# An attention and two feed-forward layers with expert routing on one core: the end of routing rearranged

## The chip, the cores and the metric

The kernel runs on one core of a Trainium2 chip. The metric is the device time of one execution in microseconds; the comparison with the kernel before is made by the median of several executions. TensorE (PE) does the matmuls and transposes here; VectorE (DVE), ScalarE (ACT) and GpSimd (POOL) work on the tiles; SyncE (SP) issues transfers. PEld in the profile is TensorE's loading of the stationary operand, which overlaps the matmuls.

## The reference

Three parts follow each other on 2304 tokens of 512 numbers (batch 4, sequence 576).

```
# 1: linear attention with random features, 8 heads
x = attention(q, k, v, omega)
# 2: normalised, gated feed-forward, 1536 wide
xn = x / sqrt(mean(x*x) + 1e-6) * rms_g
y = (silu(xn @ w_gate) * (xn @ w_val)) @ w_out
# 3: eight experts with 288 places each
logits = y @ gate                      # 2304 x 8
order = argsort(-logits.flatten())     # best pairs first
for idx in order: tok, e = idx // 8, idx % 8
    if assigned[tok] < 0 and counts[e] < 288: assigned[tok] = e; counts[e] += 1
for e in range(8): out[assigned == e] = relu(y[assigned == e] @ w1[e]) @ w2[e]
```

Everything is float32; the kernel multiplies with operands split into a high and a low part and takes three products (high by high, high by low, low by high).

## The kernel before

Attention and the first half of the feed-forward layer fill the first 556 us. The logits are known before the feed-forward's output `y` is, since the gate's weights are folded into `w_out`. So from then on two things run interleaved on PE: **routing**, a chain of many short steps that finds for each expert the threshold of its logits, and the **second half of the feed-forward layer**, `ffn2`, a generator that yields after each of its 648 matmuls (18 tiles of 128 tokens, 36 matmuls each, line 880).

Routing (`route`, lines 107 to 266) has seven phases. A phase finds a threshold in six digits; in each digit VectorE compares all logits with candidates (`ge`, line 152), PE counts the hits in 18 small matmuls (`cnt`, line 163), VectorE compares the counts with the room left (`ok`, line 165), one more matmul (line 169) sums the result, and VectorE reads the digit. The first two digits have 62 and 63 candidates, the other four 31. Then follows a settlement (lines 182 to 223). After the phases come the places of the tokens (lines 225 to 257), 18 last matmuls (line 262) and the list `ids` of the tokens of each expert (line 266). Wherever PE would wait for VectorE, `route` yields a number of nanoseconds, and the caller issues that much of `ffn2`, counted at 233 ns a matmul with the fraction carried on:

```
FILL = (5400, 2500, 1900, 466, 1400, 3400, 4500)   # first digit, second, others, ok, settlement, places, last
FILL_MM = 233
```

What is left of `ffn2` when routing ends is issued behind it (line 917). This whole stretch stands in `tc.manual_schedule(engines={PE, DVE})`: its PE and VectorE instructions keep the order in which they are written. Everywhere else a planner, which has a cost model of its own, orders each engine's instructions; every engine and every queue then works strictly in the order so made.

When a tile of `ffn2` is complete, ScalarE copies it out of PSUM into a tile `ws` (line 889) and SP stores it into `y_dr` in DRAM (line 890). SP also issues all loads. For the last two tiles (TAIL) the values are also kept in SBUF, `yt`, as a high part by ScalarE (line 886) and a low part by VectorE (line 887).

The experts work in transposed form. `gather(e, j)` (line 936) fetches 96 tokens of expert e from `y_dr` by an indirect DMA on POOL's queue, three per expert. Those of even experts go into the three tiles named `xh`, those of odd experts into the three named `xl`, of which `yt` and `hot` take up all three until expert 0 has been turned. Expert 0 does not wait for the last two feed-forward tiles: its gather reads only the earlier rows, rows that are not there are set to zero (line 942), and its four turns add the others by matmuls of `yt` with a one-hot matrix `hot` (line 957; `hot` is made on line 1001 from a loaded `iota`). `turn(e, d)` (line 944) transposes a quarter of the columns by PE into a PSUM tile `gv`, of which there are two, and splits it into `exh` by ScalarE (line 959) and `exl` by VectorE (line 960). `layer1` (line 962) makes 12 matmuls of a block of 128 hidden units, lines 968 to 970, and two evacuations (971, 972) out of one of two PSUM tiles; there are eight blocks per expert. `layer2` makes 24 matmuls per block, lines 978 to 980, and there are four blocks. `store` transposes the result back and scatters it to the output.

The experts' weights come in eight pieces of 512 KB per expert. `exp_load` (line 829) loads a piece into one of three `ws` tiles, `exp_split` (line 855) converts it into a high part (ScalarE, line 861) and a low part (VectorE, line 862) in one of twelve `wc` tiles. Six pieces are converted during routing; six `wc` tiles hold `w_out` until `ffn2` ends.

Of the kernel before, what the change touches and what calls it, by code (L numbers as in the profile page):

```python
# [1 line left out]

# [1 line left out]

# [5 lines left out]
F32 = mybir.dt.float32  # L10
# [13 lines left out]
SL = 96  # L24
# [9 lines left out]
W_SCALE = 2.0 ** -112  # L34
DIGITS = (6, 6, 5, 5, 5, 5)
SHIFTS = (26, 20, 15, 10, 5, 0)
FILL = (5400, 2500, 1900, 466, 1400, 3400, 4500)
FILL_MM = 233

DW = 3  # L40
# [239 lines left out]
def kernel(ctx, tc, qT, kT, v1, om, wgv, rms, wo, wg2, w1, w2, cfd, trd, cid, out, dbg=None):  # L280
# [548 lines left out]
    def exp_load():  # L829
        if wcur[0] < len(wseq):  # L830
            e, c = wseq[wcur[0]]
            wcur[0] += 1
            sv = stage.tile([128, 1024], F32, name="ws")
            nc.sync.dma_start(sv, w1[e, c] if c < 4 else w2[e, c - 4])
            wload[e, c] = sv
# [19 lines left out]
    def exp_split(pool, lo):  # L855
        if wcur[1] < len(wseq):
            e, c = wseq[wcur[1]]
            wcur[1] += 1
            sv = wload.pop((e, c))
            w = pool.tile([128, 2, 1024], F32R, name="wc")  # L860
            nc.scalar.copy(w[:, 0], sv)  # L861
            lo.tensor_sub(w[:, 1], sv, w[:, 0])  # L862
            wch[e, c] = w

    def ffn2():
        for i, (c, g) in enumerate(seq2):
            if i + HB - 1 < len(seq2):
                ffn2_load(*seq2[i + HB - 1])
            if i % 6 == 2 and wcur[0] < EARLY:
                exp_load()  # L870
            if i % 6 == 4 and wcur[1] < EARLY:
                exp_early()
            ht = hts.pop((c, g))
            if g == 0:
                py = psB.tile([128, DM], F32, name="py")
            for i4 in range(4):
                f = 4 * g + i4
                w = wos[f // 2].rearrange("p l (i d) -> p l i d", i=2)
                for n, (a, l) in enumerate(((0, 0), (0, 1), (1, 0))):
                    nc.tensor.matmul(py, ht[:, i4, a], w[:, l, f % 2], start=(f == 0 and n == 0),  # L880
                                     stop=(f == KF - 1 and n == 2))
                    yield
            if g == 2:
                t = c - (NC - TAIL)
                if t >= 0:
                    nc.scalar.copy(yt[t][:, 0], py)
                    nc.vector.tensor_sub(yt[t][:, 1], py, yt[t][:, 0])
                ys = stage.tile([128, DM], F32, name="ws")
                nc.scalar.copy(ys, py)  # L889
                nc.sync.dma_start(y_dr[c * 128:(c + 1) * 128, :], ys)  # L890

    yt = [xp.tile([128, 2, DM], F32R, name="xl") for _ in range(TAIL)]
    filler = ffn2()
# [40 lines left out]
    hot = xp.tile([128, TAIL, CAP], F32R, name="xl")  # L934

    def gather(e, j):
        xg[e, j] = xp.tile([SL, DM], F32, name="xl" if e % 2 else "xh")
        rows = ids[:, e * NJ + j:e * NJ + j + 1] if e else idc[:, j:j + 1]
        nc.gpsimd.indirect_dma_start(out=xg[e, j], out_offset=None, in_=y_dr if e else y_dr[:NT - 128 * TAIL, :],
                                     in_offset=bass.IndirectOffsetOnAxis(ap=rows, axis=0))  # L940
        if e == 0:
            nc.vector.tensor_scalar(xg[0, j], xg[0, j], here[:, j:j + 1], None, op0=OP.mult)

    def turn(e, d):

        if d == 0:
            xgt[e] = (sb.tile([128, KD, CAP], F32R, name="exh"), sb.tile([128, KD, CAP], F32R, name="exl"))
        xh, xl = xgt[e]
        pt = psG.tile([128, NJ, SL], F32, name="gv")
        for j in range(NJ):  # L950
            nc.tensor.matmul(pt[:, j, :], xg[e, j][:, d * 128:(d + 1) * 128], ident[:SL, :SL], is_transpose=True,
                             start=(j == 0), stop=(j == NJ - 1), skip_group_check=True)
        pv = pt.rearrange("p j s -> p (j s)")
        if e == 0:
            for t in range(TAIL):
                for l in range(2):
                    nc.tensor.matmul(pv, yt[t][:, l, d * 128:(d + 1) * 128], hot[:, t], start=False,
                                     stop=(t == TAIL - 1 and l == 1), skip_group_check=True)
        nc.scalar.copy(xh[:, d], pv)
        nc.vector.tensor_sub(xl[:, d], pv, xh[:, d])  # L960

    def layer1(e, f, hh, hl):
        xh, xl = xgt[e]
        w = wch[e, f // 2].rearrange("p l (k m) -> p l k m", k=KD)
        m = slice((f % 2) * 128, (f % 2) * 128 + 128)
        ph = ps.tile([128, CAP], F32, name="ph")
        for k in range(KD):
            nc.tensor.matmul(ph, w[:, 0, k, m], xh[:, k], start=(k == 0), stop=False)  # L968
            nc.tensor.matmul(ph, w[:, 0, k, m], xl[:, k], start=False, stop=False)  # L969
            nc.tensor.matmul(ph, w[:, 1, k, m], xh[:, k], start=False, stop=(k == KD - 1))  # L970
        nc.scalar.activation(hh[:, f], ph, AF.Relu)
        nc.vector.scalar_tensor_tensor(hl[:, f], ph, 0.0, hh[:, f], op0=OP.max, op1=OP.subtract)
# [10 lines left out]
    def store(e, j, yT):  # L983
        po = ps.tile([SL, DM], F32, name="po")
        for d in range(KD):
            nc.tensor.transpose(po[:, d * 128:(d + 1) * 128], yT[:, d, j * SL:(j + 1) * SL], ident)
        yo = sb.tile([SL, DM], F32, name="yo", bufs=3)
        nc.vector.tensor_copy(yo, po)
        nc.gpsimd.memset(spacer, 0.0)
        s_ = nc.gpsimd.indirect_dma_start(  # L990
            out=out, out_offset=bass.IndirectOffsetOnAxis(ap=ids[:, e * NJ + j:e * NJ + j + 1], axis=0),
            in_=yo, in_offset=None)
        for t in scat:
            tc.declare_no_dep(s_.ins, t.ins, reason="other rows")
        scat.append(s_)
# [9 lines left out]
    exp_load()  # L1005
    for j in range(NJ):
        gather(1, j)
    for d in range(KD):
        turn(0, d)
    w2pool = ctx.enter_context(tc.tile_pool(name="w2pool", bufs=1))  # L1010
    for n in range(2):
        exp_load()
        exp_split(wpool, nc.vector)

    yprev = None
    for e in range(E):
        hh = sb.tile([128, KE, CAP], F32R, name="ehh", bufs=1)
        hl = sb.tile([128, KE, CAP], F32R, name="ehl", bufs=1)
        yT = sb.tile([128, KD, CAP], F32, name="yT", bufs=2)
        for f in range(KE):  # L1020
            layer1(e, f, hh, hl)
            if yprev is not None and f < NJ:
                store(e - 1, f, yprev)
            if f in (3, 4, 5) and e + 2 < E:
                gather(e + 2, f - 3)
            if f % 2:
                exp_load()
                exp_split(wpool, nc.vector)
        for d in range(KD):
            if e + 1 < E:  # L1030
                turn(e + 1, d)
            layer2(e, d, hh, hl, yT)
            exp_load()
            exp_split(wpool, nc.vector)
        yprev = yT
    for j in range(NJ):
        store(E - 1, j, yprev)
# [46 lines left out]
```

## Time and profile before

| | us |
|---|---|
| median of three executions | 1009.11 (1009.09 to 1012.57) |
| profiled execution, own time | 1010.09 |
| its span from first to last instruction | 1008.2 |
| TensorE busy in the span | 971.8 |
| VectorE, ScalarE, GpSimd busy | 534.5, 399.8, 242.1 |
| first and last matmul of `ffn2` start | 556.1, 762.0 |
| first and last matmul of layer 1 of the experts start | 769.2, 984.8 |

A profile is one execution. Its page gives the busy time of each engine, the chain of work that ended last and the costliest groups of instructions; the trace behind it can be asked for the instructions of a stretch, for one source line, or for sums by window. In brackets behind an instruction stands how long its engine was idle before it and what released it. The times of matmuls overlap, since they are pipelined.

### The profile page before, as it was taken

The page shows a single profiled execution, that of the slowest core. Times are in us where ns is not written, and L with a number is a line of the kernel's source. Part 1 is how long each engine was busy: PE and PEld are TensorE (multiplying, and loading weights), DVE is VectorE, ACT ScalarE, POOL GpSimd, SP SyncE. Part 2 cuts the span into 40 slices and gives each one's busy share as a digit, 9 for nine tenths or more (in the row PEclk, how much of TensorE's full clock was granted, in tenths as well). Part 3 has the DMA queues.
Part 4 walks back from the last instruction along what each step waited for, and adds up shares of the span by engine and source line. Part 5 has one row for each costly group of instructions (what it writes and reads, how often), then busy time and mean ns, then how long its engine had stood idle before and what let it go on. Part 6 is the DMA issues. An engine that isn't in the chain of part 4 may idle for free.

```text
span 1008.2 us, 19316 instructions
## 1 busy us (share of the span) xinstructions
PE 971.8 (96%) x7649; PEld 886.8 (88%) x7649; DVE 534.5 (53%) x1239; ACT 399.8 (40%) x999; POOL 242.1 (24%) x325
## 2 busy tenths in 40 slices
PE   6998899999999999999999999999997999999996
PEld 5888899989989989999999777777776999999996
DVE  3779956544653344432234465555554656665531
ACT  4985546546654544332233100100003644444420
POOL 1345512233344222322223000000005121222111
PEclk7999999999999999999999999999998999999998
DMA  8436752366544211732224466655536755655400
GB/s 274 158 113 207 222 160 81 127 212 200 178 144 148 102 53 49 202 112 83 83 98 156 138 183 203 189 175 161 158 94 213 246 187 189 199 194 193 150 24 24
DMA packets 112074, 153.32 MB, mean 152 GB/s; under 512 B 8560, under 2 KB 78832, under 8 KB 111984
## 3 DMA queue, kind: packets, MB, share of 16 engines
q1 hardware_dynamic: 108768, 142.52, 43.8%
q0 software_dynamic: 3072, 9.44, 2.9%
q8 instruction: 60, 0.98, 0.4%
q14 instruction: 30, 0.25, 0.1%
q10 hardware_dynamic: 144, 0.13, 0.0%
HBM read 108.03 MB, written 44.04 MB: 151 GB/s over the span
## 4 chain that ended last, share of the span: by engine, by line
PE 77%; issue 9%; DVE 6%; DMA 2%; ACT 2%; POOL 2%; SPq 0%; POOLq 0%; DVEq 0%; ACTq 0%
PE py L880 16%; PE gv L595 10%; PE gv L596 9%; PE gv L597 9%; PE pm L457 3%; PE pm L412 2%; PE cnt L163 2%; PE ph L968 2%; PE py L978 2%; PE ph L970 2%; PE ph L969 2%; PE py L979 2%; PE py L980 2%; DVE dw L527 2%; PE pm L453 2%
## 5 line engine op out<-in xcount | busy, mean ns | idle before, releaser
L595 PE MATMUL gv<-xh,wc 128*128 128x256 f32 x864 | 253.5, 294 | 6.4 <-DVE hp L610 6.0
L596 PE MATMUL gv<-xl,wc 128*128 128x256 f32 x864 | 250.1, 289 | 0.0
L597 PE MATMUL gv<-xh,wc 128*128 128x256 f32 x864 | 249.7, 289 | 0.0
L880 PE MATMUL py<-wc,ht 128*128 128x512 f32 x648 | 175.9, 409 | 0.0
L595 PEld LDWEIGHTS gv<-xh,wc 128*128 128x128 f32 x864 | 165.1, 191 | 10.7 <-DVE hp L610 7.0
L596 PEld LDWEIGHTS gv<-xl,wc 128*128 128x128 f32 x864 | 165.4, 191 | 0.8
L597 PEld LDWEIGHTS gv<-xh,wc 128*128 128x128 f32 x864 | 165.4, 191 | 0.6
L880 PEld LDWEIGHTS py<-wc,ht 128*128 128x128 f32 x648 | 114.4, 188 | 21.9
L607 DVE SCALAR_TENSOR_TENSOR th<-th,gv 128x256 f32<-128x256 f32 x108 | 45.1, 418 | 122.6 <-ACT th L606 122.4
L378 ACT ACTIVATE ft<-pp,mx 128x128 f32<-128x128 f32 (+1 forms) x320 | 93.9, 373 | 25.9 <-DVE mx L375 24.7
L620 POOL TENSOR_TENSOR hp<-h,hp 128x256 fp32r<-128x256 f32 x84 | 65.5, 780 | 156.1 <-ACT hp L619 156.0
L862 DVE TENSOR_TENSOR wc<-ws,wc 128x1024 fp32r<-128x1024 f32 x58 | 70.9, 1224 | 32.7 <-ACT wc L861 32.4
L606 ACT ACTIVATE th<-gv 128x256 f32<-128x256 f32 x108 | 41.5, 384 | 105.3 <-PE gv L597 105.0
L968 PE MATMUL ph<-exh,wc 128*128 128x288 f32 x256 | 78.9, 309 | 0.0
L978 PE MATMUL py<-ehh,wc 128*128 128x288 f32 x256 | 78.0, 305 | 0.0
L970 PE MATMUL ph<-exh,wc 128*128 128x288 f32 x256 | 76.2, 298 | 0.0
L969 PE MATMUL ph<-exl,wc 128*128 128x288 f32 x256 | 76.1, 298 | 0.0
L979 PE MATMUL py<-ehl,wc 128*128 128x288 f32 x256 | 75.9, 297 | 0.0
L980 PE MATMUL py<-ehh,wc 128*128 128x288 f32 x256 | 75.8, 296 | 0.0
L375 DVE TENSOR_REDUCE mx<-pp 128x4 f32<-128x512 f32 (+2 forms) x88 | 55.6, 635 | 33.9 <-PE pp L368 21.1
L889 ACT COPY ws<-py 128x512 f32<-128x512 f32 x18 | 10.6, 586 | 145.8 <-PE py L880 132.2
L861 ACT CAST wc<-ws 128x1024 fp32r<-128x1024 f32 x58 | 61.0, 1051 | 3.1 <-DMA ws<-in_w_dram 3.0
(197 smaller groups left out, 1843.2 us busy)
## 6 DMA issues: line engine op xcount, KB each, us to landing
ws<-in_w_dram SPq DMA_DIRECT2D x64, 512.0 KB, 3.4
ht<-h_dr SPq DMA_DIRECT2D x54, 512.0 KB, 4.2
h_dr<-hp SPq DMA_DIRECT2D x42, 512.0 KB, 2.6
ws<-in_wgv_dram SPq DMA_DIRECT2D x24, 512.0 KB, 4.0
ws<-in_wo_dram SPq DMA_DIRECT2D x12, 512.0 KB, 4.3
h_dr<-dw SPq DMA_DIRECT2D x24, 256.0 KB, 2.1
y_dr<-ws SPq DMA_DIRECT2D x18, 256.0 KB, 4.3
vt<-in_v_dram SPq DMA_DIRECT2D x12, 325.0 KB, 4.0
```

Source lines behind the costliest of these rows:

```text
L378: nc.scalar.activation(ft[:n, g], pp[:n, g], AF.Exp, bias=mx[:n, g:g + 1])
L595: nc.tensor.matmul(pg[:, v], w[:, 0, k, v], xh[:, k], start=(k == 0), stop=False)
L596: nc.tensor.matmul(pg[:, v], w[:, 0, k, v], xl[:, k], start=False, stop=False)
L597: nc.tensor.matmul(pg[:, v], w[:, 1, k, v], xh[:, k], start=False, stop=(k == KD - 1))
L862: lo.tensor_sub(w[:, 1], sv, w[:, 0])
L880: nc.tensor.matmul(py, ht[:, i4, a], w[:, l, f % 2], start=(f == 0 and n == 0), stop=(f == KF - 1 and n == 2))
L968: nc.tensor.matmul(ph, w[:, 0, k, m], xh[:, k], start=(k == 0), stop=False)
L969: nc.tensor.matmul(ph, w[:, 0, k, m], xl[:, k], start=False, stop=False)
L970: nc.tensor.matmul(ph, w[:, 1, k, m], xh[:, k], start=False, stop=(k == KD - 1))
L978: nc.tensor.matmul(py, w[:, 0, k], hh[:, k], start=(k == 0), stop=False)
L979: nc.tensor.matmul(py, w[:, 0, k], hl[:, k], start=False, stop=False)
L980: nc.tensor.matmul(py, w[:, 1, k], hh[:, k], start=False, stop=(k == KE - 1))
```

## The change

`FILL` gets smaller portions for the first digit, the second and the others. The store of a finished feed-forward tile is issued by ScalarE, not by SP. The gathers of expert 1 get three tiles of their own, `xe`. An unused pool is dropped. The two conversions of weights in front of the experts' loop are dropped, so that each later one takes the piece two further back. The turns of expert 0 and all of expert 0's matmuls, with those of expert 1's turns among them, are put in the written order on PE; in that order the first two turns of expert 1 stand behind the first block of expert 0's layer 2, not before it. For the other experts the planner orders PE as before.

```diff
--- before.py
+++ after.py
@@ -1,4 +1,4 @@
-from contextlib import ExitStack
+from contextlib import ExitStack, nullcontext
 
 import numpy as np
 
@@ -34,7 +34,7 @@
 W_SCALE = 2.0 ** -112
 DIGITS = (6, 6, 5, 5, 5, 5)
 SHIFTS = (26, 20, 15, 10, 5, 0)
-FILL = (5400, 2500, 1900, 466, 1400, 3400, 4500)
+FILL = (5100, 2450, 1800, 466, 1400, 3400, 4500)
 FILL_MM = 233
 
 DW = 3
@@ -887,7 +887,7 @@
                     nc.vector.tensor_sub(yt[t][:, 1], py, yt[t][:, 0])
                 ys = stage.tile([128, DM], F32, name="ws")
                 nc.scalar.copy(ys, py)
-                nc.sync.dma_start(y_dr[c * 128:(c + 1) * 128, :], ys)
+                nc.scalar.dma_start(y_dr[c * 128:(c + 1) * 128, :], ys)
 
     yt = [xp.tile([128, 2, DM], F32R, name="xl") for _ in range(TAIL)]
     filler = ffn2()
@@ -934,7 +934,11 @@
     hot = xp.tile([128, TAIL, CAP], F32R, name="xl")
 
     def gather(e, j):
-        xg[e, j] = xp.tile([SL, DM], F32, name="xl" if e % 2 else "xh")
+        if e == 1:
+
+            xg[e, j] = sb.tile([SL, DM], F32, name="xe", bufs=NJ)
+        else:
+            xg[e, j] = xp.tile([SL, DM], F32, name="xl" if e % 2 else "xh")
         rows = ids[:, e * NJ + j:e * NJ + j + 1] if e else idc[:, j:j + 1]
         nc.gpsimd.indirect_dma_start(out=xg[e, j], out_offset=None, in_=y_dr if e else y_dr[:NT - 128 * TAIL, :],
                                      in_offset=bass.IndirectOffsetOnAxis(ap=rows, axis=0))
@@ -1005,33 +1009,37 @@
     exp_load()
     for j in range(NJ):
         gather(1, j)
-    for d in range(KD):
-        turn(0, d)
-    w2pool = ctx.enter_context(tc.tile_pool(name="w2pool", bufs=1))
-    for n in range(2):
-        exp_load()
-        exp_split(wpool, nc.vector)
+    def in_order(e):
+        return tc.manual_schedule(engines={mybir.EngineType.PE}) if e == 0 else nullcontext()
+
+    with in_order(0):
+        for d in range(KD):
+            turn(0, d)
 
     yprev = None
     for e in range(E):
         hh = sb.tile([128, KE, CAP], F32R, name="ehh", bufs=1)
         hl = sb.tile([128, KE, CAP], F32R, name="ehl", bufs=1)
         yT = sb.tile([128, KD, CAP], F32, name="yT", bufs=2)
-        for f in range(KE):
-            layer1(e, f, hh, hl)
-            if yprev is not None and f < NJ:
-                store(e - 1, f, yprev)
-            if f in (3, 4, 5) and e + 2 < E:
-                gather(e + 2, f - 3)
-            if f % 2:
+        with in_order(e):
+            for f in range(KE):
+                layer1(e, f, hh, hl)
+                if yprev is not None and f < NJ:
+                    store(e - 1, f, yprev)
+                if f in (3, 4, 5) and e + 2 < E:
+                    gather(e + 2, f - 3)
+                if f % 2:
+                    exp_load()
+                    exp_split(wpool, nc.vector)
+
+            turns = [(0,), (1,), (2,), (3,)] if e else [(), (0, 1), (2,), (3,)]
+            for d in range(KD):
+                if e + 1 < E:
+                    for t in turns[d]:
+                        turn(e + 1, t)
+                layer2(e, d, hh, hl, yT)
                 exp_load()
                 exp_split(wpool, nc.vector)
-        for d in range(KD):
-            if e + 1 < E:
-                turn(e + 1, d)
-            layer2(e, d, hh, hl, yT)
-            exp_load()
-            exp_split(wpool, nc.vector)
         yprev = yT
     for j in range(NJ):
         store(E - 1, j, yprev)
```

## Rows read from the trace of the kernel before

**Rows 1.** The page: the span, and the chain of work that ended last by engine.

```profile
span 1008.2 us, 19316 instructions
...
PE 77%; issue 9%; DVE 6%; DMA 2%; ACT 2%; POOL 2%; SPq 0%; POOLq 0%; DVEq 0%; ACTq 0%
```

**Rows 2.** Busy time in stretches: the stretch and its length, then busy us (and instructions) of PE, PEld, DVE, ACT and POOL, the granted clock of PE as a share of 2.4 GHz, the busy share of the DMA engines, GB/s.

```profile
565.00:757.00 192.00, 191.26 (x1534) 138.09 (x1533) 110.32 (x388) 15.21 (x22) 0.00 (x0) 1.00 0.56 165
...
762.39:766.66 4.27, 0.78 (x5) 0.40 (x4) 1.88 (x5) 0.87 (x2) 3.17 (x21) 1.00 0.55 197
767.13:770.07 2.94, 2.94 (x14) 2.78 (x13) 0.80 (x3) 1.01 (x3) 0.38 (x3) 0.50 0.74 255
774.75:777.37 2.62, 0.00 (x2) 0.03 (x1) 1.98 (x4) 1.49 (x3) 2.01 (x3) 0.91 0.97 308
777.37:780.31 2.94, 2.94 (x13) 2.94 (x14) 0.88 (x1) 0.00 (x0) 2.59 (x2) 0.50 0.98 309
780.31:783.31 3.00, 3.00 (x25) 2.97 (x25) 1.64 (x3) 2.31 (x5) 0.00 (x0) 1.00 0.99 284
800.00:997.00 197.00, 197.00 (x1511) 196.26 (x1511) 102.37 (x148) 84.33 (x154) 37.02 (x36) 1.00 0.47 154
```

**Rows 3.** Timeline of routing, parts of two phases: a second digit with 10 matmuls between, then a first digit with 23 and a third with 8. Columns: start in us, duration in us, engine, line, operation, tiles, shapes, count.

```profile
619.61 2.59 PE L880 MATMUL py<-wc,ht 128*128 128x512 f32 x10
620.75 1.34 DVE L152 TENSOR_TENSOR ge<-s,cand 128x1134 bf16<-128x1134 f32 x1
622.14 0.74 PE L163 MATMUL cnt<-oh,ge 128*63 128x8 bf16 x18
...
693.34 5.60 PE L880 MATMUL py<-wc,ht 128*128 128x512 f32 x23
696.24 1.32 DVE L152 TENSOR_TENSOR ge<-s,ci 128x1116 bf16<-128x1116 f32 x1
698.87 0.72 PE L163 MATMUL cnt<-oh,ge 128*62 128x8 bf16 x18
...
704.50 2.13 PE L880 MATMUL py<-wc,ht 128*128 128x512 f32 x8
705.14 0.74 DVE L152 TENSOR_TENSOR ge<-s,cand 128x558 bf16<-128x558 f32 x1
706.55 0.61 PE L163 MATMUL cnt<-oh,ge 128*31 128x8 bf16 x18
```

**Rows 4.** Timeline of the end of routing and of the turns of expert 0, all engines, same columns; SPq is the transfer queue of SP.

```profile
757.36 0.99 PE L262 MATMUL cnt<-rt,ob 128*96 128x48 bf16 x18 [1.09 <-DVE ob L257]
758.19 4.21 PE L880 MATMUL py<-wc,ht 128*128 128x512 f32 x17
...
758.55 0.33 SPq L890 DMA_DIRECT2D y_dr<-ws  x1
...
758.98 0.37 SPq L933 DMA_DIRECT2D ws<-in_tri_dram  x1
...
759.47 1.14 POOL L939 DMA_INDIRECT xh<-y_dr,idc  x1 [197.75 <-DVE idc L999]
...
762.14 0.92 POOL L939 DMA_INDIRECT xh<-y_dr,idc  x1 [0.30 <-issue]
762.43 0.58 ACT L886 CAST xl<-py 128x512 fp32r<-128x512 f32 x1 [3.91 <-PE py L880]
...
765.26 0.48 DVE L942 TENSOR_SCALAR xh<-xh,here 96x512 f32<-96x512 f32 x1 [1.52 <-DMA xh<-y_dr,idc]
765.66 0.68 DVE L887 TENSOR_TENSOR xl<-py,xl 128x512 fp32r<-128x512 f32 x1
...
766.26 0.47 DVE L942 TENSOR_SCALAR xh<-xh,here 96x512 f32<-96x512 f32 x1
766.37 0.58 ACT L889 COPY ws<-py 128x512 f32<-128x512 f32 x1 [3.36 <-DVE xl L887]
...
771.59 0.29 PE L969 MATMUL ph<-exl,wc 128*128 128x288 f32 x1
```

**Rows 5.** Timeline of the first blocks of expert 0: the gather of the first rows of expert 1, and the transpose that needs them.

```profile
773.17 0.92 POOL L939 DMA_INDIRECT xl<-y_dr,ids  x1 [0.30 <-ACT wc L861]
...
777.37 0.39 PE L951 MATMUL gv<-cf,xl 96*128 96x96 f32 x1 [2.62 <-DMA xl<-y_dr,ids]
```

**Rows 6.** Single lines of the source: the one DMA that ScalarE issues, the two copies of a turn, the low part of a weight, the low part of layer 1 (duration in ns, least, median and most; first and last start). Then three rows of the DMA issues: count, KB each, median us from issue to landing.

```profile
L706 ACTq DMA_DIRECT2D ws<-in_om_dram x1: 399/399/399, 0.7 to 0.7; - x1
...
L959 ACT CAST exh<-gv x32: 392/404/407, 768.8 to 968.2; 128x288 fp32r<-128x288 f32 x32
...
L960 DVE TENSOR_TENSOR exl<-gv,exh x32: 446/457/459, 769.2 to 968.6; 128x288 fp32r<-128x288 f32 x32
...
L862 DVE TENSOR_TENSOR wc<-ws,wc x58: 1210/1226/1261, 770.8 to 959.1; 128x1024 fp32r<-128x1024 f32 x58
...
L972 DVE SCALAR_TENSOR_TENSOR ehl<-ph,ehh x64: 445/457/460, 774.4 to 985.9; 128x288 fp32r<-128x288 f32 x64
...
y_dr<-ws SPq DMA_DIRECT2D x18, 256.0 KB, 4.3
...
xl<-y_dr,ids POOLq DMA_INDIRECT x12, 4.0
...
xh<-y_dr,ids POOLq DMA_INDIRECT x9, 5.1
```

## The prediction, made before the changed kernel was run

> **What bounds the kernel now.** I read the page first: PE makes 77% of the chain that ended last [rows 1], so only what shortens PE's own sequence, or a stretch in which PE waits, can move the end. The change touches the time from the start of routing on, so next I cut that time into windows [rows 2]. From 565 to 757 us (routing with feed-forward between its steps) PE is busy 191.26 of 192.00 us: PE is what every step there ends on. From 800 to 997 us (experts 1 to 7) it is busy 197.00 of 197.00 us; nothing can be won there, only lost. Between them lie two holes: 762.39 to 766.66 us with 0.78 us of work, and 774.75 to 777.37 us with none. Each is followed by 2.94 us at a granted clock of 0.50, the lower of PE's two levels (1.2 GHz), and PE had been idle before both falls. That is where something is to be had.
>
> Then the timeline of single steps [rows 3]. The reader is to compare the end of the `ge` comparison (start plus duration) with the start of the counting matmuls that need it. In a first step `ge` ends at 696.24 + 1.32 = 697.56, counting starts at 698.87: 23 feed-forward matmuls hold the chain up for 1.31 us. In a step of digits 2 to 5 it is 706.55 − 705.88 = 0.67 us with 8 matmuls; in a second step with 10 matmuls 622.14 − 622.09 = 0.05 us, which is the bare handover. One matmul costs (5.60 − 2.13) / 15 = 0.23 us. So the portions are too long for the chain by one to five matmuls in all steps but the second.
>
> Last the hand-over to the experts [rows 4, 5]: the last feed-forward matmul ends at 762.40, but gather 3 was only issued at 762.14, its rows were scaled at 766.26, and VectorE, in its order, kept the last feed-forward tile's low half (L887) behind the wait for gather 2 until 765.66. Expert 0's matmuls run without a break from 771.45 (771.59 is the start of the first recorded one) until 774.75, where a transpose of expert 1 stands in PE's order and waits 2.62 us for its rows, gathered at 773.17 only.
>
> **The smaller portions.** `fill` carries fractions, so I ran its arithmetic with both lists: 631 of the 648 feed-forward matmuls are issued before the last routing matmuls now (17 are left, as the row of 17 shows [rows 4]), 609 afterwards, 39 left. Of the 22 that move, two come out of the very first step, which already waits for VectorE, and give nothing. The other 20 come out of steps with 0.28 us or more to spare (a second step that gets 11 in place of 10 pays 0.23, one that goes the other way gains it; both are in the count; portion 6 loses one and portion 7 gains one, and both wait for VectorE either way). 20 × 0.23 = 4.6 us: the last routing matmuls move from 757.36 to 752.8. PE's total work is the same, so feed-forward ends at 762.40 + 22 × 0.23 − 4.6 = 762.9, half a microsecond later than now. By itself this edit gives nothing; it lets the gathers run beside PE work. Bounds: 0 to 4.6 us of routing, and I take 4.6.
>
> **Turn of expert 0.** The gathers keep their pace, so the third is issued at 762.14 − 4.6 = 757.5 and lands by the second's delay now (issue 1.2 us earlier, scaled at 765.26) at about 761.7, scaled at 762.2; with 5.1 us to landing, the slower median [rows 6], it would be 763.1. Either is over before the new last in line, the last feed-forward tile: ScalarE's cast 762.9 to 763.5 (0.58), VectorE's L887 to 764.2 (0.68), then the last `yt` matmul of turn 0 ends at 764.4. A turn is 7 PE instructions at 3.00 / 25 = 0.12 us [rows 2], 0.8 us. Turn 1 ends at 765.2. Turn 2 needs turn 0's PSUM buffer back.
>
> **The stores on ScalarE's queue.** Each issue takes 0.33 us on SP now; the one DMA that ScalarE issues today took 0.40 [rows 6], so 18 × 0.40 = 7 us of a ScalarE that is 15.21 us busy in 192 [rows 2]; hidden, but for the last. That one stands in ScalarE's order behind the copy L889 (764.25 to 764.84), and the casts of expert 0 stand behind it: L959 from 765.25 to 765.65, L960 to 766.15 [rows 6]. Turn 2 therefore starts at 766.2, a microsecond after turn 1 ended, turn 3 ends at 767.8. If the planner puts L959 ahead of the store, it is 0.9 us less; that is the other bound. The Trainium skill ("TensorE: Matmul & The Clock Gate", on engine queue depths) says that ScalarE's and VectorE's queues are strict first in, first out; the rows agree on VectorE, where L887 stood ready and waited 2.6 us. By that rule the move makes ScalarE a place where a store holds back casts; without it one would put turn 3's end at 766.9.
>
> On SP's queue the store no longer holds back what follows: the iota load left at 758.98 right after the store at 758.55 [rows 4]. Its tile is needed by the `hot` comparisons only, which are then early. Price 0; the feed-forward loads behind the stores show no wait of PE in 192 us.
>
> So expert 0's dense stretch starts at 767.8, against 771.45 less two matmuls done early (0.27), 771.2: **3.4 us**.
>
> **Own tiles for expert 1's rows, and PE's order by hand in expert 0.** Its three gathers need the last store (issued at 765.25, landing 4.3 us later, 769.6), and POOL's three issues and 4.0 us of landing [rows 6]: about 777. The transposes now come after 96 matmuls of layer 1 and 24 of layer 2, at 767.8 + 120 × 0.13 (197.00 us / 1511 [rows 2]) = 783.4. The wait of 2.62 us goes, with 6 us to spare, and with it the low clock behind it, half of 2.94: 1.5 us. Together **4.1 us**. What takes its place: layer 1 in strict order has two PSUM buffers, and VectorE's L972 (0.46) can lie behind a weight subtraction (1.23) [rows 6]. Per pair of blocks PE needs 3.2 us, VectorE 2 × 0.46 + 1.23 = 2.1; an unlucky order costs some 0.13 us a pair, at most 0.45 a block. I take **−0.5 us** (0 to −3.6).
>
> **Weight conversion later.** The seventh and eighth piece are converted behind the second and fourth block, not before the first. A conversion is 2.3 us, the seventh piece is needed at the third block of layer 2, 96 + 48 matmuls or 19 us after the start: covered by 13 us. It also takes the 1.23 us subtraction out of the turn's copies. Price 0; without the cover, 2.3 us.
>
> **Sum.** 3.4 + 4.1 − 0.5 = 7.0 us. Made against the profiled execution (1010.09 us, 1.9 more than its span of 1008.2) that is 1003.1; the median of the runs shown is 1009.11, 1.0 below it, so I forecast **1002.1 us**. By the bounds: 1000.6 with the better order and no stall.
>
> **Rivals.** (1) *Expert 0's turn still makes PE wait.* The forecast leaves PE short of work for 1.5 of the 3.4 us after 762.9. If the clock falls as at both holes now, 2.94 us at half speed cost 1.5; a copy of a turn behind a weight subtraction costs up to 1.2 more, a late gather something over that: 1003.6 to 1006. For it: both holes ended that way, the second after 2.62 us. Against: a hole this time has matmuls inside. The Trainium skill ("TensorE: Matmul & The Clock Gate", Part 1) calls the low clock the default that activity lifts; the two falls agree with it, and by it a partly idle turn may be enough. Chance 0.22. (2) *The portions free nothing*, since something other than those matmuls holds the steps: 39 matmuls end at 767.5, expert 0 starts at 772.4, and 4.1 − 0.5 − 1.2 = 2.4 us remain: 1006.7. Against: the step gaps follow the number of matmuls, 0.05 and 0.67. Chance 0.06. (3) *Slower: the planner lays out experts 1 to 7 anew and badly.* Conversion runs two pieces later, so every copy of a turn meets another neighbour; one that lands behind a 1.23 us subtraction with PE waiting, in half of the 28 turns, costs 17 us: 1019. It decides from 12 / 28 = 0.43 us a turn on. For it: the same planner put the transpose of 774.75 where its rows could not be. Against: PE lost nothing in 197 us with VectorE busy 102 and ScalarE 84. Chance 0.07.
>
> **Chances and range.** Forecast 0.62 (1000.6 to 1003.6), the three rivals 0.35, the rest unnamed. Half a per cent, about what a measurement of this kernel tells from no change, is 5.0 us, so faster by more means under 1004.1: the forecast and a quarter of rival 1, 0.67. Rival 2 and the rest of rival 1 are within 0.5%: 0.25. Slower 0.08. The range, 1000.6 to 1006.0, takes the forecast and rival 1.
>
> **What would show it.** Right: `ge` ends within 0.1 to 0.5 us of counting in digits 2 to 5 and 1.1 in first steps; L262 near 753; 39 feed-forward matmuls behind it; PE's wait in expert 0's turn ends on L887, then on L960; no PE wait for expert 1's rows; clock 1.00 from 775 to 785. Wrong: a PE wait over 1 us between 765 and 800, a clock of 0.50 there, or gaps of PE between experts after 800.

## The result and the profile after

The changed kernel takes 1019.06 us (median; 1015.42 to 1021.13) where the kernel before took 1009.10 beside it: a ratio of 1.0089 [1.0061, 1.0118], slower by 9 us by that ratio (10 by the two medians) where 7 us faster was forecast. A second series on another chip gave 1018.31 us and 1.0062 [1.0041, 1.0083] (changed_again in the tables below). The profiled execution, the longest of the four, took 1021.13 us for a span of 1019.3. About 3 us of that lie ahead of the change: feed-forward's first weight load starts at 558.95, before at 555.97, behind code that is the same. So stages are compared from that start below.

The line numbers have moved: a turn's matmuls are L955 and L961 and its copies L963 (ScalarE) and L964 (VectorE); a block of layer 1 is L972 to L974 and its copies L975 (ScalarE) and L976 (VectorE); the conversion of a weight is still L861 (ScalarE) and L862 (VectorE).

The page, its span and chain, against [rows 1]: DMA has gone from 2 to 4% of the chain, DVE from 6 to 7.

```profile
span 1019.3 us, 19307 instructions
...
PE 75%; issue 9%; DVE 7%; DMA 4%; ACT 2%; POOL 2%; SPq 0%; POOLq 0%; ACTq 0%; DVEq 0%
```

Busy time in stretches, columns as in [rows 2]:

```profile
565.00:757.00 192.00, 190.44 (x1560) 137.44 (x1559) 112.83 (x394) 14.63 (x21) 0.00 (x0) 1.00 0.58 168
757.00:767.00 10.00, 8.98 (x41) 7.12 (x39) 3.10 (x9) 1.76 (x3) 3.66 (x11) 1.00 0.44 138
767.00:777.00 10.00, 7.15 (x34) 6.37 (x34) 4.18 (x8) 4.39 (x7) 5.03 (x21) 0.67 0.59 187
777.00:800.00 23.00, 16.85 (x90) 15.71 (x91) 11.70 (x15) 9.23 (x16) 6.38 (x6) 0.77 0.88 256
800.00:1008.00 208.00, 208.00 (x1598) 207.29 (x1597) 108.05 (x155) 90.13 (x165) 34.96 (x33) 1.00 0.45 149
```

The loss lies between 767 and 800 us alone: PE is busy 24.0 of 33 us, and at a mean clock well under 1. Behind 800 PE is full, as before. The same stretch cut at the changes of the clock (length, PE's busy time and matmuls, clock, DMA share, GB/s):

```profile
767.00:770.31 3.31, 1.98 (x12) 1.00 0.44 123
770.31:783.96 13.65, 10.83 (x44) 0.50 0.85 253
783.96:794.20 10.24, 5.80 (x41) 1.00 0.91 251
794.20:797.60 3.40, 2.99 (x13) 0.50 0.67 251
```

At the lower level PE worked 10.83 + 2.99 = 13.8 us, of which half, 6.9, is lost; before it was half of 2 × 2.94 [rows 2]. PE had been idle for 1.3 of the 3.3 us ahead of the first fall, and had waited 1.85 us (until 792.80) ahead of the second.

The end of routing and the turns of expert 0, against [rows 4]:

```profile
755.59 0.99 PE L262 MATMUL cnt<-rt,ob 128*96 128x48 bf16 x18 [0.87 <-DVE ob L257]
...
756.42 9.30 PE L880 MATMUL py<-wc,ht 128*128 128x512 f32 x39
...
766.38 0.69 DVE L887 TENSOR_TENSOR xl<-py,xl 128x512 fp32r<-128x512 f32 x1 [2.19 <-ACT xl L886]
...
767.50 0.78 PE L961 MATMUL gv<-xl 128*128 128x288 f32 x4 [1.52 <-DVE xl L1005]
767.72 0.33 ACTq L890 DMA_DIRECT2D y_dr<-ws  x1
```

39 feed-forward matmuls now stand behind the last routing matmuls, as forecast, and the wait of 2.62 us for expert 1's rows [rows 5] is gone. In its place stand these waits of PE between 757 and 800 us (who waits, for whom: us, times, longest):

```profile
PE ph L972 <- DVE ehl L976: 4.8, 3, 2.6
PE ph L972 <- ACT exh L963: 2.0, 2, 1.6
PE gv L961 <- DVE xl L1005: 1.5, 1, 1.5
PE gv L955 <- DVE exl L964: 0.9, 1, 0.9
PE ph L973 <- DVE exl L964: 0.7, 1, 0.7
```

All but the third are for copies of a turn or of a block. ScalarE's timeline shows why these are late:

```profile
768.10 1.05 ACT L861 CAST wc<-ws 128x1024 fp32r<-128x1024 f32 x1 [0.41 <-ACT ws L889]
769.05 0.69 ACT L963 CAST exh<-gv 128x288 fp32r<-128x288 f32 x2
771.72 1.05 ACT L861 CAST wc<-ws 128x1024 fp32r<-128x1024 f32 x1 [1.98 <-DMA ws<-in_w_dram]
772.68 0.39 ACT L963 CAST exh<-gv 128x288 fp32r<-128x288 f32 x1
776.19 1.04 ACT L861 CAST wc<-ws 128x1024 fp32r<-128x1024 f32 x1 [3.12 <-DMA ws<-in_w_dram]
777.14 0.39 ACT L963 CAST exh<-gv 128x288 fp32r<-128x288 f32 x1
779.35 1.05 ACT L861 CAST wc<-ws 128x1024 fp32r<-128x1024 f32 x1 [1.82 <-DMA ws<-in_w_dram]
780.30 0.41 ACT L975 ACTIVATE ehh<-ph 128x288 fp32r<-128x288 f32 x1
...
786.35 1.04 ACT L861 CAST wc<-ws 128x1024 fp32r<-128x1024 f32 x1 [3.23 <-DMA ws<-in_w_dram]
787.30 0.40 ACT L975 ACTIVATE ehh<-ph 128x288 fp32r<-128x288 f32 x1
```

A conversion stands in front of nearly every copy, and it waits for its load. The fourth `gv` was ready at about 774.1 (the last L961 started in the group of 772.77 and 1.31 us), but its copy ran at 777.14, right behind the conversion of 776.19, which had waited 3.12 us for its 512 KB. PE's L972 then waited 1.59 us for that copy. At 786.35 the same happens to a block: the conversion has waited 3.23 us for its load, L975 follows at 787.30, VectorE's subtraction and L976 follow that, and PE starts again at 789.07 after 2.58 us. Six pieces of expert 0 had been converted during routing; what is converted here are its last two, which the end of layer 2 needs, and then those of expert 1.

In the kernel before, too, a conversion stands in front of most copies of blocks. The difference is how many stand ahead of the first one:

```profile
769.75 1.05 ACT L861 CAST wc<-ws 128x1024 fp32r<-128x1024 f32 x1
...
772.08 1.05 ACT L861 CAST wc<-ws 128x1024 fp32r<-128x1024 f32 x1
773.52 0.41 ACT L971 ACTIVATE ehh<-ph 128x288 fp32r<-128x288 f32 x1 [0.38 <-PE ph L970]
...
775.95 1.04 ACT L861 CAST wc<-ws 128x1024 fp32r<-128x1024 f32 x1 [0.75 <-DMA ws<-in_w_dram]
```

Two conversions ran there ahead of the first block's copy, and the fourth began 220.0 us after feed-forward's first weight load. Now four run ahead of it, and the fourth begins at 220.4, no earlier, since its load is no earlier. So the copy came at 217.55 before and comes at 221.35 now, although PE reaches expert 0 2.7 us earlier.

The group of conversions on the page, of after and then of before (instructions, busy us, mean ns, idle time ahead of them and what ended it):

```profile
L861 ACT CAST wc<-ws 128x1024 fp32r<-128x1024 f32 x58 | 60.9, 1051 | 15.2 <-DMA ws<-in_w_dram 14.7
```

```profile
L861 ACT CAST wc<-ws 128x1024 fp32r<-128x1024 f32 x58 | 61.0, 1051 | 3.1 <-DMA ws<-in_w_dram 3.0
```

14.7 us against 3.0 (10.6 in changed_again). ScalarE has that much idle time to give; what it has not is another way for the copies behind.

The stages, worked out from the traces, in us after feed-forward's first weight load: start of the last routing matmuls, end of feed-forward's last weight load (its last matmul ends 0.4 us later), start of the first weight load of layer 1 of experts 0, 1 and 2, end of the span.

```
                      L262   ffn end  expert 0  expert 1  expert 2   end
before               201.39   205.99   213.26    246.14    274.28   452.19
after                196.64   206.35   210.54    254.43    282.57   460.39
changed_again        196.65   206.35   210.55    251.27    279.41   457.24
free_order           196.72   206.42   210.05    248.24    276.34   454.20
portions_alone       196.72   206.46   210.09    245.61    273.75   451.57
three_in_order       196.65   206.36   211.12    241.48    271.69   453.58
earlier_loads        196.64   206.39   210.59    247.05    275.18   453.10
all_in_order         196.71   206.42   211.18    238.87    267.02   444.99
copies_in_order      196.74   206.44   210.08    240.22    268.35   446.30
copies_again         196.71   206.41   210.05    238.75    266.89   444.84
ordered_old_portions 201.36   205.97   213.88    250.06    278.21   456.15
old_portions_again   201.36   205.97   212.95    242.66    270.80   448.74
```

Expert 0 takes 254.43 − 210.54 = 43.9 us where it took 32.9; everything else is as forecast or as before. How much it loses differs between executions: in changed_again, the same kernel, it takes 40.7.

### The profile page after: what moved, and what is told of

It is laid out like the page before. It is cut to its first block, busy times and chain, and to the rows that moved or that the text cites. A ratio compares the mean times of both kernels' runs of the same rounds, so it can differ in the third digit from the quotient of the medians.

```text
span 1019.3 us, 19307 instructions
## 1 busy us (share of the span) xinstructions
PE 977.3 (96%) x7649; PEld 891.3 (87%) x7649; DVE 534.7 (52%) x1239; ACT 399.0 (39%) x999; POOL 240.9 (24%) x325
## 4 chain that ended last, share of the span: by engine, by line
PE 75%; issue 9%; DVE 7%; DMA 4%; ACT 2%; POOL 2%; SPq 0%; POOLq 0%; ACTq 0%; DVEq 0%
PE py L880 15%; PE gv L595 9%; PE gv L596 9%; PE gv L597 9%; PE pm L457 3%; PE pm L412 2%; PE cnt L163 2%; PE py L982 2%; PE py L983 2%; PE py L984 2%; DMA ws<-in_w_dram 2%; DVE dw L527 2%; PE ph L972 2%; PE ph L974 2%; PE ph L973 2%
## 5 line engine op out<-in xcount | busy, mean ns | idle before, releaser
L378 ACT ACTIVATE ft<-pp,mx 128x128 f32<-128x128 f32 (+1 forms) x320 | 93.9, 373 | 27.7 <-DVE mx L375 26.3
L862 DVE TENSOR_TENSOR wc<-ws,wc 128x1024 fp32r<-128x1024 f32 x58 | 71.0, 1224 | 44.1 <-ACT wc L861 44.1
L972 PE MATMUL ph<-exh,wc 128*128 128x288 f32 x256 | 80.5, 314 | 6.8 <-DVE ehl L976 4.8
L974 PE MATMUL ph<-exh,wc 128*128 128x288 f32 x256 | 77.9, 304 | 0.0
L861 ACT CAST wc<-ws 128x1024 fp32r<-128x1024 f32 x58 | 60.9, 1051 | 15.2 <-DMA ws<-in_w_dram 14.7
L889 ACT COPY ws<-py 128x512 f32<-128x512 f32 x18 | 10.6, 587 | 139.6 <-PE py L880 135.1
```

Source lines behind the costliest of these rows:

```text
L378: nc.scalar.activation(ft[:n, g], pp[:n, g], AF.Exp, bias=mx[:n, g:g + 1])
```

## The experiments

Ratios are to the kernel before on the same chip, with a 95% interval. Where the copies of ScalarE and VectorE are called in written order, the source puts, per expert, the turn's copies, then two blocks of layer 1, one conversion, and so on.

**free_order.** The changed kernel, with PE's order and the turns of expert 1 as before.

```
-        return tc.manual_schedule(engines={mybir.EngineType.PE}) if e == 0 else nullcontext()
+        return nullcontext()
-            turns = [(0,), (1,), (2,), (3,)] if e else [(), (0, 1), (2,), (3,)]
+            turns = [(0,), (1,), (2,), (3,)]
```

> The changed kernel with the written order on PE taken out of expert 0 (the planner orders PE there as before, the first two turns of expert 1 stand where they stood); portions, stores on ScalarE's queue, own tiles and later conversion stay. Theory A (queue order): with PE in written order the planner put a weight conversion ahead of the copies of expert 0 on ScalarE and VectorE, each conversion waits there for its load, and PE waits behind the copies and falls to the low clock. Without the written order the planner's ScalarE order is that of the kernel before (two copies of a turn first, then a conversion), so the loss goes and the 4.7 us of routing stay: 1003 to 1006 us, PE's waits on ehl and exh in expert 0 under 3 us together. Theory B (the early gathers of expert 1 and the stores on the other queue slow down the weight loads): the loads stay late, 1014 us or more. Theory C (later conversion is what lacks): 1014 us or more as well.

1011.59 us, 1.0015 [0.9990, 1.0041]. ScalarE's conversions wait only 3.5 us for loads, and PE no longer waits for copies of blocks. Two conversions stand ahead of the first block's copy, as in before. So it is what the change does to PE's order that makes the planner put more of them in front; which half of it, the written order or the late place of expert 1's first turns, is not told, since this run takes out both. The expected 1003 to 1006 us were missed all the same, for without the two the transposes of expert 1 stand too early:

```profile
PE gv L955 <- DMA xe<-y_dr,ids: 6.3, 3, 3.8
```

PE's clock stood at 0.50 for 10.24 us around these waits (771.79 to 782.03), and expert 0 takes 38.2 us.

**portions_alone.** The kernel before with the new `FILL`, nothing else.

> The kernel before with the smaller portions alone. Theory A: the portions are good by themselves; the last routing matmuls come 4.7 us earlier, expert 0's turn follows the end of feed-forward more closely, the wait for expert 1's rows (2.6 us) and its low clock stay: 1009.1 less 3 to 4, 1005 to 1006. Rival E (the earlier end of routing only moves the wait, since the loads of weights start no earlier): 1008 to 1010.

1009.23 us, 0.9990 [0.9976, 1.0003]. Routing ends 4.67 us earlier, and expert 0 starts 3.2 us earlier; then PE meets the same transpose, and the wait of 2.62 us [rows 5] has grown:

```profile
PE gv L951 <- DMA xl<-y_dr,ids: 4.6, 1, 4.6
```

The transpose starts only 1.4 us earlier than in before (219.97 us after feed-forward's first weight load, there 221.40), so most of what was won is waited away: the end is 0.6 us earlier.

**three_in_order.** The changed kernel, with ScalarE and VectorE in written order too in expert 0.

```
-        return tc.manual_schedule(engines={mybir.EngineType.PE}) if e == 0 else nullcontext()
+        return tc.manual_schedule(engines={mybir.EngineType.PE, mybir.EngineType.Activation, mybir.EngineType.DVE}) if e == 0 else nullcontext()
```

> The changed kernel with ScalarE and VectorE, too, in written order in expert 0, so that a conversion stands behind every second block of layer 1 and behind no copy of a turn. Theory A: PE keeps its written order and no longer waits for copies behind conversions: expert 0 takes 27 to 28 us from its first to expert 1's first matmul (40 or so in the changed kernel), 1001 to 1004 us in all. Rival D (a strictly written order on PE is itself what costs, since PE can pull nothing ahead while an evacuation is late): PE still waits on ehl for 5 us or more, 1010 us or more. Theory B: the loads come as late as in the changed kernel, and the conversions, wherever they stand, hold up the evacuations: 1010 us or more.

1010.29 us, 0.9993 [0.9973, 1.0014]. Expert 0 takes 30.4 us instead of 43.9, which shows the order of the copies as the cause there. But experts 1 and 2 now take 30.2 and 32.2 us where each other kernel needs 28.1: the planner, free again, catches up with the conversions there, and they wait for loads:

```profile
825.64 1.05 ACT L861 CAST wc<-ws 128x1024 fp32r<-128x1024 f32 x1 [1.79 <-DMA ws<-in_w_dram]
...
827.18 1.06 ACT L861 CAST wc<-ws 128x1024 fp32r<-128x1024 f32 x1
...
830.84 1.05 ACT L861 CAST wc<-ws 128x1024 fp32r<-128x1024 f32 x1 [2.30 <-DMA ws<-in_w_dram]
```

**earlier_loads.** The changed kernel with two further tiles for loads, used by two pieces in five.

```
-            sv = stage.tile([128, 1024], F32, name="ws")
+            if wl and wcur[0] % 5 < 2:
+                sv = wl[0].tile([128, 1024], F32, name="wl")
+            else:
+                sv = stage.tile([128, 1024], F32, name="ws")
```

> The changed kernel with two more tiles for the loads of the experts' weights (pieces go in turn into five tiles, not three), so that two more loads are issued ahead of the end of routing; the order of conversions and copies on ScalarE and VectorE stays that of the changed kernel but for one conversion in layer 1. Theory A: the order costs only because each conversion waits for its load; with the loads there earlier ScalarE's 14.7 us of waiting on weight loads fall to a third and with them most of the loss: 1005 to 1010 us. Rival F (not the wait but the work of conversions in front of copies costs, 1.05 us on ScalarE and 1.23 us on VectorE for each): no more than 3 us come back, 1015 us or more.

1011.68 us, 1.0009 [0.9989, 1.0030]: the order stays nearly as in after (five conversions ahead of the first block's copy, where after has four), the loads are issued earlier, the conversions wait 5.2 us instead of 14.7 or 10.6, and most of the loss is back: in the stages 7.3 of the 8.2 us of after, or 4.1 of the 5.1 us of changed_again. So both are needed for the loss: a conversion in front of the copies, and a load that is late.

**all_in_order** and **copies_in_order.** Written order in all experts, on all three engines or on ScalarE and VectorE alone.

```
-        return tc.manual_schedule(engines={mybir.EngineType.PE}) if e == 0 else nullcontext()
+        return tc.manual_schedule(engines={mybir.EngineType.PE, mybir.EngineType.Activation, mybir.EngineType.DVE})
```

> The changed kernel with PE, ScalarE and VectorE in written order in all experts: a conversion behind every second block of layer 1 and behind every block of layer 2, one per 3.2 us of PE's work, never more. Theory G (catching up): once feed-forward ends, six weight tiles come free, and the planner converts as fast as tiles come free, with each copy of the experts behind a conversion that waits for its load; three load tiles of about 4 us to landing and 2.3 us of conversion give one piece in 2.1 us at best, less beside the gathers, so PE follows the loads until the twelve tiles are full, and what routing gained is paid back there. With the conversions spread evenly the loads keep up: no wait of ScalarE on a weight load above 1 us in total, experts 28.2 us each, 1001 to 1004 us. Rival H (the bytes themselves are late: 190 KB gathers and 512 KB loads in the first 30 us of the experts take the DMA engines whatever the order): PE loses 5 us or more in experts 0 to 2 and the time stays at 1008 to 1010.

> The same with ScalarE and VectorE alone in written order in all experts; PE's order is the planner's. Theory G: the conversions no longer hold up copies; what is left is where the planner puts the turns of expert 1 on PE, ahead of rows that land 14 us after the end of feed-forward: a wait of 0 to 4 us, 1002 to 1007. Rival D (the strict order on PE is what costs): faster than the version with PE in written order as well, by 2 us or more.

1003.20 us, 0.9936 [0.9917, 0.9954], and 1000.55 us, 0.9925 [0.9892, 0.9957]. Both beat the two kernels of the study, before by 0.6 and 0.8%. In all_in_order no conversion waits for a load:

```profile
L861 ACT CAST wc<-ws 128x1024 fp32r<-128x1024 f32 x58 | 60.6, 1046 | 0.0
```

and the stretch that was full of holes is closed, at a clock of 1.00:

```profile
767.00:777.00 10.00, 10.00 (x76) 9.87 (x75) 5.02 (x8) 4.70 (x10) 6.89 (x6) 1.00 0.66 210
777.00:800.00 23.00, 23.00 (x180) 22.98 (x180) 13.26 (x19) 11.49 (x21) 5.44 (x5) 1.00 0.61 202
```

Its end is 452.19 − 444.99 = 7.2 us earlier than before's, and PE's written order is in it: that order by itself costs nothing that these intervals can tell.

**conversions_back** and **shared_rows.** The changed kernel with one part undone each: the two conversions back in front of the loop, or the rows of expert 1 in the shared tiles.

```
+    for n in range(2):
+        exp_load()
+        exp_split(wpool, nc.vector)
```

```
-        if e == 1:
-            xg[e, j] = sb.tile([SL, DM], F32, name="xe", bufs=NJ)
-        else:
-            xg[e, j] = xp.tile([SL, DM], F32, name="xl" if e % 2 else "xh")
+        xg[e, j] = xp.tile([SL, DM], F32, name="xl" if e % 2 else "xh")
```

> The changed kernel with the two conversions ahead of the experts' loop put back; its order of conversions and copies on ScalarE and VectorE up to the end of expert 1 is that of the changed kernel. Theories A and G: the later conversion was not what cost, 1016 to 1021 us as the changed kernel. Rival C (later conversion): 1011 or less.

> The changed kernel with expert 1's rows in the shared tiles again; the order of conversions and copies is unchanged. Theories A and G: 1016 to 1021, no difference clear of noise, since the transposes of expert 1 come 25 us later anyhow. Theory B (the gathers of expert 1, no longer held back by the turns, take the DMA engines from the weight loads): 3 us or more faster, and the loads in the first 20 us land 2 us earlier.

1017.60 us, 1.0074 [1.0047, 1.0100], and 1014.78 us, 1.0048 [1.0030, 1.0067]. Where the source writes the two conversions is no cause: the planner lays ScalarE out in the same order, and the conversions wait 15.1 us. The own tiles show no part either: without them ScalarE waits 10.8 us for loads and expert 0 takes 40.4 us, with them 10.6 and 40.7 in changed_again, and the intervals overlap.

**changed_again** and **order_alone.** The changed kernel once more (given above), and the kernel before with the copies in written order.

```
+        return tc.manual_schedule(engines={mybir.EngineType.Activation, mybir.EngineType.DVE})
```

> The changed kernel once more, on the chip of the three below. Both theories expect what it took: 1015 to 1021 us; with it the version with shared rows (1014.8) is to be judged.

> The kernel before with ScalarE and VectorE in written order in all experts and nothing else of the change (old portions, stores on SP, shared tiles, the two early conversions, old places of the turns). Theory G: catching up costs the kernel before, too, but there it lies beside the waits for expert 1's rows, which stay; two or three us at most come back, 1006 to 1009. Rival I (the written order of the copies is all that helps, the four edits are worth nothing): 1000 to 1003.

order_alone: 1011.27 us, 1.0000 [0.9987, 1.0014]. The 2 or 3 us expected did not come back. The waits of before stand in its trace untouched, 3.4 us for the late rows of expert 0's turn and 2.6 for expert 1's. The order wins nothing by itself; it only lets through what the change wins.

**ordered_old_portions** and **ordered_shared_rows.** copies_in_order with the old `FILL`, or with the shared tiles.

> The version with ScalarE and VectorE in written order in all experts (1000.6 us) with the old portions. Theory: with the order cured the 4.7 us of routing are worth what the prediction said of expert 0's turn, some 3.4 us: 1003 to 1005. Rival I: no difference, 1000 to 1002.

> The same version with expert 1's rows in the shared tiles: its gathers wait for expert 0's turn. The version's PE has the transposes behind the first block of layer 2, so rows that come 1 or 2 us later are not waited for: 1000 to 1002. Rival: the own tiles are what lets the turns of expert 1 be on time: 1003 or more, with a wait of PE for these rows.

1013.92 us, 1.0015 [0.9996, 1.0035], and 1004.45 us, 0.9931 [0.9906, 0.9956]. The second says that own tiles are worth nothing that can be told once the transposes stand late. The first was a surprise, 9 us over the expectation, and its trace shows copies that ScalarE makes late though their matmuls are done:

```profile
777.45 0.41 ACT L975 ACTIVATE ehh<-ph 128x288 fp32r<-128x288 f32 x1 [2.51 <-PE ph L974]
777.75 1.04 ACT L861 CAST wc<-ws 128x1024 fp32r<-128x1024 f32 x1
783.12 0.71 ACT L975 ACTIVATE ehh<-ph 128x288 fp32r<-128x288 f32 x2 [4.33 <-remote]
```

So it was repeated, on one chip with its partner and with the one part that no run had undone.

**copies_again, old_portions_again** and **sp_stores_ordered.** The last is copies_in_order with

```
-                nc.scalar.dma_start(y_dr[c * 128:(c + 1) * 128, :], ys)
+                nc.sync.dma_start(y_dr[c * 128:(c + 1) * 128, :], ys)
```

> The changed kernel with the copies of ScalarE and VectorE in written order in all experts, PE's order left to the planner, once more. If its earlier 1000.6 us (ratio 0.9925) was no accident of its series: 0.990 to 0.996 of before, expert 0 in 28 us.

> The same with the old portions of feed-forward. Theory A (the portions are worth what the prediction gave them, and the earlier 1013.9 us was one of a disturbed series): 1003 to 1006 us, ratio 0.995 to 0.998, expert 0 in 28 to 30 us. Theory B (they are worth more than that, since routing's end shifts what the gathers, the loads and the copies of expert 0 meet): 1012 to 1015 us, ratio near 1.002, expert 0 in about 36 us with ScalarE's copies late by 2 us and more between 773 and 785.

> The copies in written order, the new portions, but the feed-forward's stores back on SP's queue. Theory C (the stores' queue is worth nothing, as its price of 0.9 us at most says): 0.990 to 0.996, within 1 us of copies_again. Theory D (the last store on SP's queue holds up the weight loads of expert 0 or on ScalarE's keeps its casts back): over 2 us off, slower in the first case, faster in the second.

1000.63 us, 0.9905 [0.9880, 0.9929]; 1004.63 us, 0.9951 [0.9930, 0.9972]; 1000.78 us, 0.9910 [0.9884, 0.9936]. The portions are worth 4.0 us (3.9 in the stages), and the earlier 1013.92 was not repeated. The stores' queue is worth nothing: both traces end 444.84 us after feed-forward's start. The old portions show what the new ones take away, the wait for the rows of expert 0's turn:

```profile
PE gv L955 <- DVE xh L946: 3.1, 3, 1.7
```

Around this wait the clock stood at 0.50 for 6.83 us (761.93 to 768.76); in copies_again it does not fall.

## Why the prediction was wrong

**The smaller portions: right.** Forecast 4.6 us of routing and feed-forward 0.5 later; measured 201.39 − 196.64 = 4.75 and 0.36. Of the signs, the 1.1 us of first steps came (1.07 to 1.09). That for digits 2 to 5 held in 8 steps of 28: counting starts 0.67 us behind `ge` in the 20 where 8 matmuls still stand between, 0.44 where 7 do.

**The turn of expert 0: right in size, where the copies are on time.** The dense stretch was to start 3.4 us earlier. In the stages' time it starts at 215.62 in before and at 212.25 in all_in_order, 3.37 earlier. On the way two steps were off: `hot` (L1005) was not early but stood behind L887 on VectorE, so PE's wait of 1.52 us ended there; and the last store on ScalarE's queue, from which the term had up to 0.9 us, holds back nothing (sp_stores_ordered).

**Own tiles and PE's order: right in size, wrong in part.** The wait of 2.62 us is gone in every kernel with the late transposes, and the low clock behind it, 4.1 us together, where the copies are on time. It is the transposes' place that does it; ordered_shared_rows has no such wait either.

**The whole sum.** 3.4 + 4.1 − 0.5 = 7.0 us; all_in_order has 7.2 and copies_again 7.35 in the stages. copies_in_order, the kernel of copies_again in an earlier series, has 5.9: there the clock stood at 0.50 for 3.41 us of work (763.21 to 766.62), behind the wait of 1.3 us for `hot`; copies_again has the same wait without the fall. The sum holds for kernels whose copies are on time, and these are not the kernel that was forecast.

**The step that failed** is the price of conversions in front of copies, in two paragraphs. The one on PE's order by hand asked what takes the place of the wait and counted only the 1.23 us of a subtraction in front of L972, "at most 0.45 a block": −0.5 us. "Weight conversion later" expected conversions to leave the turn's copies and asked only when a converted weight is needed: "covered by 13 us", "Price 0". Neither asked what stands behind a conversion on ScalarE and VectorE while it waits for its load. (That the source writes the two conversions later costs nothing by itself, as conversions_back shows.) The prediction took for granted that a conversion has its load, and that the planner, of whose PE order the change takes a part away, would leave the two copying engines as they were. Neither held. By the stages expert 0 pays 11.0 us more than before (7.8 in changed_again), where −0.5 was allowed. Of the 43.9 us, 8.4 are waits of PE for copies (4.8 + 2.0 + 0.9 + 0.7) and 6.9 low clock; all_in_order takes 27.7, and 27.7 + 8.4 + 6.9 = 43.0. The Trainium skill ("TensorE: Matmul & The Clock Gate", on engine queue depths) was weighed in the prediction only for the store; the rows at 776.19 and 777.14 show the same strict order, at 3.12 us in one place, for an instruction that nobody needed soon.

**The rivals.** The third, slower, gave 1019 us with a chance of 0.07: the time was met by luck. Its mechanism (the planner lays out copies anew, behind conversions) was near, but its place was wrong. Experts 1 to 6 take 28.1 us each, as before; the loss is in expert 0, and it comes from conversions that wait for their loads, not from the 1.23 us of a subtraction. The first rival had the place and the signs (PE waits in expert 0's turn, a copy behind a weight conversion, the clock falls, here at 770.31), but priced such a copy at 1.2 us and so ended at 1006. The signs named for "wrong" appeared as written: waits over 1 us between 765 and 800, and a clock of 0.50.

**What stays open.** Why the planner puts more conversions ahead when PE's order is changed is not shown, nor whether the written order or the late transposes bring it, only that it does with both (after, conversions_back) and does not without (free_order). What released ScalarE 4.33 us late in ordered_old_portions is not known either.

## What to carry to other kernels

An instruction that can wait for a DMA has to be priced by what stands behind it on its engine, not by when its result is due: here conversions whose results nobody needed yet held back the copies that PE waited for. When one engine's order is changed by hand, look at the orders of all engines that feed it: here the planner laid out the rest anew, and an edit that is worth 7 us can cost 9. A gain at one place is only had if the next wait does not move with it (portions_alone); and a surprising time is repeated in another series before it is explained.

## What the runs showed of the hardware

Gathers of the same experts can take twice as long to land. The DMA issues of after between 757 and 800 us (count, KB each, median us to landing): the gathers of experts 1 to 3 take 7.4 to 8.3 us, while the DMA engines are 0.85 to 0.91 busy at 251 to 253 GB/s. In the same 43 us they take 3.2 to 5.0 in all_in_order, whose weight loads are spread out (0.61 to 0.66 busy), but also only 4.7 and 5.8 in before, where the engines are 0.97 to 0.99 busy at 284 to 309 GB/s (774.75 to 783.31 [rows 2]). So a busy share does not tell the landing time; what does is not shown.

```profile
ws<-in_w_dram SPq DMA_DIRECT2D x12, 512.0 KB, 4.7
y_dr<-ws ACTq DMA_DIRECT2D x2, 256.0 KB, 3.6
xh<-y_dr,idc POOLq DMA_INDIRECT x3, 3.3
xe<-y_dr,ids POOLq DMA_INDIRECT x3, 7.7
xh<-y_dr,ids POOLq DMA_INDIRECT x3, 7.4
xl<-y_dr,ids POOLq DMA_INDIRECT x3, 8.3
```

Issuing a store costs ScalarE 0.33 us, as on SP, not the 0.40 that the one row of before had suggested [rows 6]. And two series of one kernel, each with a narrow interval, gave 1.0015 and 0.9951: between chips and series more differs than the interval of one shows.
